# Attention's 64-row query block moved from the end of the sequence to its start, and shorter fills of the expert rows

## The chip, the cores and the metric

The kernel runs on one core of a Trainium2 chip. The metric is the device time of one execution in microseconds (us); below it the profile's own span, from the first to the last instruction, is used to read where the time lies. TensorE is called PE in the profile (PEld is its weight load), VectorE DVE, ScalarE ACT, GpSimd POOL, and SyncE, which issues most transfers, SP.

## The reference

Three layers run one after the other, all in float32. The change touches the first one and the scratch rows of the second.

```python
# attention: B, H, S, D = 4, 8, 576, 64
scores = scale * q @ k.T                      # scale = 1/sqrt(D)
cum = cumsum(maximum(s, 0), axis=-1)
bias = -(cum[:, :, :, None] - cum[:, :, None, :])
scores = where(causal, -1e9, scores + minimum(bias, 0.0))
attn = softmax(scores)                        # with + 1e-9 in the denominator
x = (attn @ v) -> rows of 512                 # B * S = 2304 rows
# mixture of experts: one of 8 experts for each row
e = argmax(x @ w_gate); y = gate * (relu(x @ w1[e]) @ w2[e])
# gated layer
out = (silu(xn @ w_gate) * (xn @ w_val)) @ w_out      # xn: y normalized by its rms
```

The sequence has 576 = 4.5 x 128 rows, and a query row sees only the keys up to its own place.

## The kernel before

The 32 heads are worked in 16 pairs `p`, two heads `h` side by side in the 128 partitions (64 for each head). For each pair these steps run, each a function that issues instructions of one kind:

- `attn_load`, `load_bias`, `load_v`: SP's transfers of q, k, the cumulated `s` (broadcast over partitions: `sums` for the full blocks, `cm` for the short block) and v.
- `mask_sums`, `q_diag`: on POOL, from pair 2 on, the causal mask is added to the bias, and the short block's queries of both heads are laid out block-diagonally (`bd`).
- `s_mm` (with `s_start`): PE makes the scores of a query block `i`, and DVE reads them from PSUM, adds the bias and takes the row's extreme (`reduced`, line 298). The full blocks 0 to 3 (128 rows each) see 128, 256, 384 and 512 keys; each is a pair of matmuls, one for each head, which contract over that head's 64 partitions. The short block `sm` (block 4, rows 512 to 575) puts 64 rows of either head into one block of 128 rows and contracts over all 128 partitions; it sees all 576 keys, in two halves of 288.
- `s_exp`: ACT's nine exponentials of a pair. `s_norm`: the reciprocals of the sums, on DVE.
- `t_mm`: PE transposes the probabilities in 25 blocks of 128 x 128, gathered in seven PSUM tiles t0 to t6, and ACT copies them to `pt` in ten copies (line 406).
- `pv_mm`: the product with v, `pvy` for rows 64 to 575 and `pvx` for the first 64, over five key blocks j. `pv_out`: two copies on ACT. `o_mm`: PE multiplies by identity and gate weights (`tl`), DVE scales into `xt` and `lp`.

The order on PE, ACT, DVE and SP is the order of the code: `attention` makes a plan of (time, function) from the tables `POS`, `TURN` and others, in units in which a pair is 10 long, sorts it and issues. Steps of different pairs overlap: PE runs the scores of pair p+1, then the transposes of pair p, then `sm` of p+1, then the product of pair p. PSUM has eight banks under one tag, and every tile takes one in turn, so a tile waits until the one eight places ahead has been read.

`route` (one call for each of the four batches) ranks the rows by expert and scatters them with an indirect DMA on POOL to `xs`, in which each expert has its own region. Before that `prefill` writes empty rows at the head of each of the eight regions: 384 rows (`FILLR`) from one row of zeros, `zrow`. The next stage reads at most 312 rows (`CAP[0]`) of a region other than the first.

After attention the expert stage runs on PE (lines 915 and 938), then the gated layer (lines 1320, 1713 and 1778).

## Time and profile before

| | |
|---|---|
| median of 3 runs | 839.19 us (838.82 to 839.22) |
| the profiled execution's own time | 838.61 us |
| its span, first to last instruction | 836.9 us |
| mean granted TensorE clock | 0.994 of full |
| PE / DVE / ACT / POOL busy | 98% / 76% / 55% / 27% of the span |

Attention takes about the first 180 us of the span. What is outside the span is 838.61 - 836.9 = 1.7 us. Busy time of PE is modelled: neighbouring matmuls overlap, so the time that a group costs is read from the chain of waits or from the distance between starts rather than from the sum of its instructions.

### The profile page before, as it was taken

The page shows a single profiled execution, that of the slowest core. Times are in us where ns is not written, and L with a number is a line of the kernel's source. Part 1 is how long each engine was busy: PE and PEld are TensorE (multiplying, and loading weights), DVE is VectorE, ACT ScalarE, POOL GpSimd, SP SyncE. Part 2 cuts the span into 40 slices and gives each one's busy share as a digit, 9 for nine tenths or more (in the row PEclk, how much of TensorE's full clock was granted, in tenths as well). Part 3 has the DMA queues.
Part 4 walks back from the last instruction along what each step waited for, and adds up shares of the span by engine and source line. Part 5 has one row for each costly group of instructions (what it writes and reads, how often), then busy time and mean ns, then how long its engine had stood idle before and what let it go on. Part 6 is the DMA issues. An engine that isn't in the chain of part 4 may idle for free.

```text
span 836.9 us, 15788 instructions
## 1 busy us (share of the span) xinstructions
PE 816.7 (98%) x5622; PEld 746.7 (89%) x5622; DVE 639.6 (76%) x1425; ACT 461.9 (55%) x1060; POOL 227.0 (27%) x249
## 2 busy tenths in 40 slices
PE   7999999999999999999999999999999999999994
PEld 4777767789899999999999999999999998899994
DVE  6657688965866768777698988988888869868880
ACT  5988989865756656566543433333333334553440
POOL 3335856332000000000221233444343351031120
PEclk9999999999999999999999999999999999999997
DMA  7999989236567566767661332322222376344510
GB/s 226 299 320 314 315 245 295 84 126 214 193 193 245 179 228 204 237 206 233 225 197 66 131 109 103 131 94 98 104 100 99 108 282 191 81 151 146 159 52 29
DMA packets 79757, 146.72 MB, mean 175 GB/s; under 512 B 7424, under 2 KB 44315, under 8 KB 79667
## 3 DMA queue, kind: packets, MB, share of 16 engines
q1 hardware_dynamic: 76707, 136.08, 51.4%
q0 software_dynamic: 2912, 9.46, 3.0%
q8 instruction: 46, 0.75, 0.4%
q14 instruction: 44, 0.36, 0.1%
q10 hardware_dynamic: 48, 0.07, 0.0%
HBM read 108.04 MB, written 37.54 MB: 174 GB/s over the span
## 4 chain that ended last, share of the span: by engine, by line
PE 92%; DVE 3%; ACT 2%; DMA 1%; issue 1%; SPq 0%; POOL 0%; POOLq 0%; DVEq 0%; ACTq 0%
PE gg L1320 29%; PE g L938 12%; PE g L915 12%; PE gp L1778 10%; PE go L1713 6%; PE pvy L419 5%; PE t L373 5%; PE s L310 5%; PE tl L447 2%; PE sm L341 1%; PE xp L886 1%; ACT pt L406 1%; DMA ringa<-ytd 1%; PE r L987 1%; PE r L976 1%
## 5 line engine op out<-in xcount | busy, mean ns | idle before, releaser
L938 PE MATMUL g<-h,u 128*128 128x256 f32 (+7 forms) x768 | 104.3, 294 | 0.0
L915 PE MATMUL g<-xt,u 128*128 128x256 f32 (+7 forms) x768 | 103.9, 294 | 0.0
L915 PEld LDWEIGHTS g<-xt,u 128*128 128x128 f32 x768 | 101.0, 188 | 0.8
L938 PEld LDWEIGHTS g<-h,u 128*128 128x128 f32 x768 | 100.5, 188 | 0.5
L1297 POOL TENSOR_TENSOR ws<-raw,ws 128x512 fp32r<-128x512 f32 (+1 forms) x25 | 33.0, 1335 | 219.4 <-ACT ws L1292 219.4
L747 ACT CAST u<-raw 128x1024 fp32r<-128x1024 f32 x62 | 65.1, 1050 | 20.9 <-DMA raw<-in_w 20.9
L354 ACT ACTIVATE p<-sc,nm 128x128 f32<-128x128 f32 (+3 forms) x128 | 71.2, 581 | 6.0 <-DVE nm L298 6.0
L760 DVE TENSOR_TENSOR u<-raw,u 128x1024 fp32r<-128x1024 f32 x58 | 70.3, 1216 | 0.9 <-ACT u L747 0.9
L1320 PE MATMUL gg<-gx2a,ws 128*128 128x384 f32 x360 | 67.4, 335 | 0.6 <-DVE tmp L1342 0.6
L1320 PE MATMUL gg<-gx0a,ws 128*128 128x384 f32 x360 | 67.7, 336 | 0.0
L1320 PE MATMUL gg<-gx1a,ws 128*128 128x384 f32 x360 | 67.1, 335 | 0.0
L1320 PEld LDWEIGHTS gg<-gx2a,ws 128*128 128x128 f32 x360 | 62.8, 188 | 0.9 <-DVE tmp L1342 0.9
L1320 PEld LDWEIGHTS gg<-gx0a,ws 128*128 128x128 f32 x360 | 63.1, 188 | 0.0
L1320 PEld LDWEIGHTS gg<-gx1a,ws 128*128 128x128 f32 x360 | 62.7, 188 | 0.0
L1358 POOL TENSOR_TENSOR hs<-tmp,hs 128x384 f32<-128x384 f32 x27 | 30.3, 1122 | 106.2 <-ACT hs L1356 106.2
L406 ACT COPY pt<-t 128x512 f32<-128x512 f32 (+3 forms) x160 | 56.0, 451 | 3.0 <-PE t L373 2.0
L373 PE MATMUL t<-ident,p 128*128 128x128 f32 x400 | 52.1, 275 | 0.1
L373 PEld LDWEIGHTS t<-ident,p 128*128 128x128 f32 x400 | 44.5, 140 | 8.5 <-DVE nm L298 8.3
L1699 POOL DMA_INDIRECT out<-raw,oid x18 | 20.5, 1138 | 112.1 <-DVE raw L1800 64.5
L419 PE MATMUL pvy<-pt,vp 128*64 128x512 f32 (+4 forms) x320 | 47.5, 428 | 0.9 <-ACT pt L406 0.9
L1338 ACT COPY tmp<-gg 128x384 f32<-128x384 f32 x27 | 13.0, 482 | 57.1 <-PE gg L1320 55.4
L1248 ACT ACTIVATE raw<-raw 128x512 f32<-128x512 f32 x31 | 21.1, 681 | 36.0 <-DVE raw L1246 35.8
(391 smaller groups left out, 1809.5 us busy)
## 6 DMA issues: line engine op xcount, KB each, us to landing
raw<-in_w SPq DMA_DIRECT2D x64, 512.0 KB
hd<-hs SPq DMA_DIRECT2D x72, 192.0 KB
xs<-zrow SPq DMA_DIRECT2D x8, 771.0 KB
raw<-in_wo SPq DMA_DIRECT2D x12, 512.0 KB
raw<-in_wg SPq DMA_DIRECT2D x12, 512.0 KB
raw<-in_wv SPq DMA_DIRECT2D x12, 512.0 KB
vp<-in_v SPq DMA_DIRECT2D x16, 320.0 KB
in<-cumd SPq DMA_DIRECT2D x20, 256.0 KB
```

Of the source, the lines that this page charges most:

```text
L310: k.nc.tensor.matmul(ps[h], st.q[r, 128 * i:128 * i + 128], st.k[r, 0:w], start=True, stop=p >= BYPE)
L354: k.nc.scalar.activation(out, st.s[i, h][:, 0:w], AF.Exp, bias=st.nm[:, n:n + 1], scale=-1.0, accum_out=acc)
L373: nc.tensor.transpose(ps[:, off:off + 128], src[:, 128 * j:128 * j + 128], k.ident)
L406: nc.scalar.copy(b, a)
L419: nc.tensor.matmul(st.y[r, a - 64:512], st.v[:, h, j, :], k.pt[:, h, o:o + S - a], start=j == 0, stop=j == 4)
L747: nc.scalar.copy(w[:, :, 0, :], raw)
L760: k.nc.vector.tensor_tensor(w[:, :, 1, :], raw, w[:, :, 0, :].bitcast(F32), op=ALU.subtract)
L915: nc.tensor.matmul(ps[:, 0:n], w[:, f % 4, a, 128 * kc:128 * kc + 128], x[b][:, kc, 0:n], start=kc == 0 and i == 0, stop=kc == 3 and i == 2)
L938: nc.tensor.matmul(ps[:, 0:n], w[:, f % 4, a, 128 * c:128 * c + 128], k.h[b][:, f, 0:n], start=f == 0 and i == 0, stop=f == 7 and i == 2)
L1320: k.nc.tensor.matmul(k.ps[u, bank], w[:, a, 128 * c:128 * c + 128], x[:, b, GT * c:GT * c + GT], start=first and c == 0 and n == 0, stop=c ...
L1713: k.nc.tensor.matmul(k.acc[tau], c[:, a, 128 * t:128 * t + 128], w[:, b, :], start=f == 0 and i == 0, stop=f == NF - 1 and i == 2)
L1778: k.nc.tensor.matmul(k.acc[i, bank], t[:, a, j, :], item_weight(k, j, w, b), start=first and j == 0 and n == 0, stop=j == 5 and n == 2, sk ...
```

## The change

The short block becomes block 0: queries 0 to 63, which see 64 keys. The full blocks become 1 to 4 and start 64 rows in, so that they see 192, 320, 448 and 576 keys. The widest one does not fit into a PSUM bank and is made in two halves of 288. A half block of 64 keys is left at the end of each full block's row; head 1's probabilities are stored with their 64-key blocks in reverse order, so that the half blocks of the two heads lie side by side and are transposed together (v of head 1 is laid out to match by the host). The mask adds on POOL change with it, `cm` needs 64 instead of 576 columns, and the row tile that has only 64 rows is the first instead of the last. The tables give the steps their new order. `zrow`, `mz` and `half` move into free columns of the probability buffers. `prefill` writes 312 rows (104 partitions x 3) in seven of the eight regions.

```diff
-JB = (0, 576, 1024, 1344, 1536)
+STRIP = (1408, 0, 448, 896, 1344)
+START_OF = [128 * i * i - 128 for i in range(5)]
+UNITS64, C0, LAST = 16, 4, 13
...
+    n = CM // 3 if c else FILLR // 3
     i = nc.sync.dma_start(
-        out=k.xs[REG * c:REG * c + FILLR, :].rearrange("(a p) d -> p a d", p=128),
-        in_=k.zrow.unsqueeze(1).broadcast_to((128, FILLR // 128, XROW)),
+        out=k.xs[REG * c:REG * c + 3 * n, :].rearrange("(a p) d -> p a d", p=n),
+        in_=k.zrow[0:n].unsqueeze(1).broadcast_to((n, 3, XROW)),
...
     if n == 0:
-        in_turn(k, G.tensor_tensor(cb[:, :, 0:2, :], cb[:, :, 3:1:-1, :], m.unsqueeze(1).broadcast_to(sh), op=ALU.add))
-        in_turn(k, G.tensor_tensor(cb[:, :, 5, :], cb[:, :, 5, :], m.broadcast_to((128, 2, 128)), op=ALU.add))
+        in_turn(k, add(cb[:, :, LAST:16, :], cb[:, :, C0:C0 + 3, :], 1))
+        in_turn(k, add(cb[:, :, C0 - 1::-1, :], cb[:, :, C0 + 1:C0 + 5, :], 0))
+        in_turn(k, add(cb[:, :, C0 + 7:LAST, :], cb[:, :, C0 + 7:LAST, :], 2))
...
-        k.nc.sync.dma_start(out=st.cm[64 * h:64 * h + 64, :], in_=k.cumd[2 * p + h:2 * p + h + 1, :].broadcast_to((64, S)))
+        k.nc.sync.dma_start(out=st.cm[64 * h:64 * h + 64, :], in_=k.cumd[2 * p + h:2 * p + h + 1, 0:64].broadcast_to((64, 64)))
...
+def width(i):
+    return 64 + 128 * i
...
+def s_start(k, p, i, c=0, w=None):
+    st, w = k.st[p], w or width(i)
+    q = slice(128 * i - 64, 128 * i + 64)
+    ps = st.ps[i, c] = [bank(k, f"s{p}_{i}_{c}_{h}", w) for h in range(2)]
     for h, r in enumerate(ROWS2):
-        k.nc.tensor.matmul(ps[h], st.q[r, 128 * i:128 * i + 128], st.k[r, 0:w], start=True, stop=p >= BYPE)
+        k.nc.tensor.matmul(ps[h], st.q[r, q], st.k[r, c:c + w], start=True, stop=p >= BYPE or c + w < width(i))
...
     if i == 0:
+        ps = bank(k, f"sm{p}", 64)
+        nc.tensor.matmul(ps, st.bd, st.k[:, 0:64], start=True, stop=False)
+        nc.tensor.matmul(ps, k.identb, k.mask[:, 0, 0:64], start=False, stop=True)
+        reduced(k, scores(0)[:, 0:64], ps, st.cm, acc(10))
...
+    else:
+        for c in (HALF, 0):
+            s_start(k, p, 4, c, HALF)
...
-            ps = k.psum.tile([128, 512], F32, name=f"sm{p}_{n}", tag="b")[:, 0:HALF]
-            nc.tensor.matmul(ps, st.bd, st.k[:, c], start=True, stop=n == 0)
...
+        if h:
+            out, src = (t.rearrange("p (b n) -> p b n", n=64) for t in (out, src))
+            out = out[:, ::-1, :]
...
-TURN = dict(S=(0, 1, 3, 2, 4), X=(0, 1, 2, 3, 6, 7, 4, 5, 8))
+TURN = dict(S=(1, 2, 4, 3, 0), X=(0, 1, 2, 3, 6, 7, 4, 5, 8))
```

Three places show what moves. First PE's matmuls for the scores of pair 2, before (a row names the tile written, with block and head, and its shape; `in` holds q and k):

```order
L310 MATMUL s_0_0_430<-in_143 128x128
L310 MATMUL s_0_1_431<-in_143 128x128
L310 MATMUL s_1_0_439<-in_143 128x256
L310 MATMUL s_1_1_440<-in_143 128x256
L310 MATMUL s_3_0_454<-in_143 128x512
L310 MATMUL s_3_1_455<-in_143 128x512
L310 MATMUL s_2_0_462<-in_143 128x384
L310 MATMUL s_2_1_463<-in_143 128x384
...
L341 MATMUL sm_0_535<-in_143 128x288
L341 MATMUL sm_1_538<-in_143 128x288
L343 MATMUL sm_1_538<-mask,identb 128x64
```

The same steps of pair 2 on PE after the change (a full block's third number is the first key of the half):

```order
L328 MATMUL s_1_0_0_441<-in_144 128x192
L328 MATMUL s_1_0_1_442<-in_144 128x192
L328 MATMUL s_2_0_0_450<-in_144 128x320
L328 MATMUL s_2_0_1_451<-in_144 128x320
L328 MATMUL s_4_288_0_464<-in_144 128x288
L328 MATMUL s_4_288_1_465<-in_144 128x288
L328 MATMUL s_4_0_0_468<-in_144 128x288
L328 MATMUL s_4_0_1_469<-in_144 128x288
L328 MATMUL s_3_0_0_481<-in_144 128x448
L328 MATMUL s_3_0_1_482<-in_144 128x448
...
L354 MATMUL sm_553<-in_144 128x64
L355 MATMUL sm_553<-mask,identb 128x64
```

Per head the full blocks go from 1280 to 1536 columns and from four tiles to five; the short block goes from 2 x 288 to 64 columns. Next ACT's copies of the transposed probabilities of pair 1 to `pt`, before:

```order
L406 COPY pt_154<-t_1_488 128x512
L406 COPY pt_154<-t_2_495 128x384
L406 COPY pt_154<-t_3_502 128x384
L406 COPY pt_154<-t_4_507 128x2x256
L406 COPY pt_154<-t_5_513 128x2x128
L406 COPY pt_154<-t_5_513 128x2x2x64
L406 COPY pt_154<-t_6_520 128x2x64 x3
```

And after the change:

```order
L453 COPY pt_149<-t_1_507 128x512
L453 COPY pt_149<-t_2_514 128x384
L453 COPY pt_149<-t_3_521 128x384
L453 COPY pt_149<-t_4_526 128x2x256
L453 COPY pt_149<-t_5_532 128x2x128
L453 COPY pt_149<-t_5_532 64x64 x2
L453 COPY pt_149<-t_6_539 64x4x64 x2
```

With the copy of t0 ahead of these rows it is ten copies before and after. Before, `pvy`'s first matmul pair (j = 0, 512 columns) read t0, t1 and the second copy of t5; after, it reads t0 and t1 alone, `pvx` reads the small copies of t5, and j = 1 is the first that reads t6. Last POOL's mask adds of one pair (pair 4), before:

```order
L249 TENSOR_TENSOR cb_148<-cb_148,mz 128x2x256
L250 TENSOR_TENSOR cb_148<-cb_148,mz 128x2x128
L253 TENSOR_TENSOR cb_148<-cb_148,mz 128x256 x2
...
L249 TENSOR_TENSOR in_142<-in_142,mz 128x2x256
L250 TENSOR_TENSOR in_142<-in_142,mz 128x2x128
```

And after:

```order
L258 TENSOR_TENSOR cb_147<-cb_147,p_129 128x2x192
L258 TENSOR_TENSOR cb_147<-cb_147,p_129 128x2x4x64
L258 TENSOR_TENSOR cb_147<-cb_147,p_129 128x2x128
...
L259 TENSOR_TENSOR cb_147<-cb_147,p_129 128x128 x2
L293 TENSOR_TENSOR in_144<-in_144,p_129 128x128
```

The adds ahead of the pair's scores become three (384, 512 and 256 columns) instead of two (512 and 256); the two that stand between a pair's reductions shrink from 256 to 128 columns.

## Rows read from the trace of the kernel before

**Rows 1.** The page: busy time, and the span in 40 slices.

```profile
PE 816.7 (98%) x5622; PEld 746.7 (89%) x5622; DVE 639.6 (76%) x1425; ACT 461.9 (55%) x1060; POOL 227.0 (27%) x249
...
DMA  7999989236567566767661332322222376344510
```

**Rows 2.** Busy time by windows: attention, one stretch of it, the expert stage.

```profile
20.00:180.00 160.00, 158.71 (x1237) 112.86 (x1236) 115.93 (x498) 144.30 (x458) 82.12 (x90) 1.00 0.86 263
80.00:100.00 20.00, 19.70 (x152) 13.83 (x150) 11.99 (x55) 19.02 (x60) 16.20 (x17) 1.00 1.00 330
300.00:470.00 170.00, 170.00 (x1215) 167.50 (x1214) 133.13 (x206) 95.05 (x185) 18.00 (x14) 1.00 0.59 191
```

**Rows 3.** The chain of waits over one pair: start, duration, what.

```profile
162.17 2.36 PE s L310 x16
...
167.14 0.76 PE t L373 x7
...
168.40 0.97 PE sm L341 x4
169.37 0.03 PE sm L343
169.40 0.33 PE tl L447 x2
169.72 1.01 PE pvy L419 x4
170.73 0.12 PE pvx L423 x4
170.85 1.73 PE pvy L419 x16
172.58 0.26 PE t L373
```

**Rows 4.** The timeline at an ordinary pair's scores, from 43.6 us.

```profile
43.76 2.43 PE L310 MATMUL s<-in,in 64*128 64x128 f32 x16
...
44.42 0.29 DVE L298 CUSTOM_DVE_ANT_0 sc<-s,cb 128x128 f32<-128x128 f32 x1 [1.95 <-PE s L310]
...
44.85 0.42 DVE L298 CUSTOM_DVE_ANT_1 sc<-s,cb 128x256 f32<-128x256 f32 x1
```

**Rows 5.** The timeline at a pair whose bias came late, from 64.7 us.

```profile
64.72 2.43 PE L310 MATMUL s<-in 64*128 64x128 f32 x16
...
65.10 1.27 POOL L249 TENSOR_TENSOR in<-in,mz 128x512 f32<-128x512 f32 x1 [6.70 <-DMA in<-cumd]
...
66.41 0.29 DVE L298 CUSTOM_DVE_ANT_0 sc<-s,in 128x128 f32<-128x128 f32 x1 [2.59 <-POOL in L249]
```

**Rows 6.** Groups of instructions by form, 23.4 to 180 us: PEld, PE, ACT, POOL.

```profile
L373 PEld LDWEIGHTS t<-ident,p 128*128 128x128 f32 x375 | 41.8, 141 | 8.4 <-DVE nm L298 8.3
...
L419 PE MATMUL pvy<-pt,vp 128*64 128x512 f32 x60 | 16.2, 618 | 0.7 <-ACT pt L406 0.7
...
L354 ACT ACTIVATE p<-sc,nm 128x512 f32<-128x512 f32 x28 | 21.6, 770 | 0.0
...
L354 ACT ACTIVATE p<-sc,nm 128x128 f32<-128x128 f32 x28 | 11.1, 404 | 4.7 <-DVE nm L298 4.7
...
L250 POOL TENSOR_TENSOR in<-in,mz 128x256 f32<-128x256 f32 x10 | 7.4, 738 | 0.0
```

**Rows 7.** The chain of waits at the start, 12 to 22 us.

```profile
15.10 2.71 ACT p L354 x11
17.81 2.72 ACT pt L406 x7
...
20.58 1.08 PE pvy L419 x4
```

**Rows 8.** The page, DMA issues: KB each.

```profile
xs<-zrow SPq DMA_DIRECT2D x8, 771.0 KB
...
in<-cumd SPq DMA_DIRECT2D x22, 144.0 KB
```

More of the change, by code (lines that the diff above doesn't have):

```diff
@@ L158, in cumulate @@
     yield
-    for i in range(2):
+    for i in (1, 2):
         s_start(k, 0, i)
@@ new lines, in scores, with acc @@
+    def scores(h):
+        sc = st.s[i, h] = A.tile([128, S], F32, name=f"sc{p}_{i}_{h}", tag="sc", bufs=4)
+        return sc
+    def acc(n):
+        return st.nm[:, n:n + 1]
+    if i == 1:
+        st.nm = A.tile([128, 12], F32, name=f"nm{p}", tag="nm", bufs=3)
+    w = width(i)
+    if i == 0:
+        ps = bank(k, f"sm{p}", 64)
+        nc.tensor.matmul(ps, st.bd, st.k[:, 0:64], start=True, stop=False)
+        nc.tensor.matmul(ps, k.identb, k.mask[:, 0, 0:64], start=False, stop=True)
+        reduced(k, scores(0)[:, 0:64], ps, st.cm, acc(10))
+    elif i < 4:
+        if (i, 0) not in st.ps:
+            s_start(k, p, i)
+        ps = st.ps.pop((i, 0))
+        if p < BYPE:
+            mask_pe(k, ps, w)
+        for h in range(2):
+            sc, a = scores(h)[:, 0:w], acc(2 * i - 2 + h)
+            c = st.cb[:, h]
+            if p < BYPE or i == 3:
+                reduced(k, sc, ps[h], sums(st, h)[:, 0:w], a)
+            elif i == 1:
+                reduced(k, sc, ps[h], flat(c[:, LAST:16, :]), a)
+            else:
+                reduced(k, *(t.rearrange("p (b n) -> p b n", n=64) for t in (sc, ps[h])), c[:, C0::-1, :], a)
+    else:
+        for c in (HALF, 0):
+            s_start(k, p, 4, c, HALF)
+        if p < BYPE:
+            mask_pe(k, st.ps[4, HALF], HALF)
+        sc = [scores(h) for h in range(2)]
+        for c in (HALF, 0):
+            ps = st.ps.pop((4, c))
+            for h in range(2):
+                reduced(k, sc[h][:, c:c + HALF], ps[h], sums(st, h)[:, c:c + HALF], acc((8 if c else 6) + h))
+                if c and p >= BYPE:
+                    mask_sums(k, p, 1 + h)
+        nc.vector.tensor_tensor(st.nm[:, 6:8], st.nm[:, 6:8], st.nm[:, 8:10], op=ALU.min)
@@ L387, in t_mm, with both @@
+    def both(a, n):
+        return ps[:, a:a + 2 * n].rearrange("p (h n) -> p h n", h=2)
+    ev = []
+    if g < 4:
+        j, h = divmod(g, 2)
+        for i in range(j + 1, 5):
+            tr(128 * (i - j - 1), i, h, j)
+        n = 512 - 128 * j
+        a = STRIP[j] + 64
+        ev.append((ps[:, 0:n], pt[:, h, a:a + n]))
     elif g == 4:
         for h in range(2):
-            for i in range(2, 4):
-                tr(256 * h + 128 * (i - 2), ph[i][h], 2)
-        ev.append(both(0, 4, JB[2]))
+            for i in (3, 4):
+                tr(256 * h + 128 * (i - 3), i, h, 2)
+        ev.append((both(0, 256), pt[:, :, STRIP[2] + 64:STRIP[2] + 320]))
@@ new lines, in t_mm @@
+        nc.tensor.transpose(ps[0:64, 256:384], pm, k.ident)
+        ev.append((both(0, 128), pt[:, :, STRIP[3] + 64:STRIP[3] + 192]))
+        for h in range(2):
+            ev.append((ps[0:64, 256 + 64 * h:320 + 64 * h], pt[64 * h:64 * h + 64, h, STRIP[0]:STRIP[0] + 64]))
+    else:
+        for i in range(1, 5):
+            a = START_OF[i] + 128 * i
+            nc.tensor.transpose(ps[:, 128 * i - 128:128 * i], ph[:, a:a + 128], k.ident)
+        for h in range(2):
+            ev.append((ps[64 * h:64 * h + 64, :].rearrange("p (i n) -> p i n", i=4)[:, :, 64:128],
+                       pt[64 * h:64 * h + 64, h, 0:1792].rearrange("p (i n) -> p i n", i=4)[:, :, 0:64]))
```

149 lines of the change are left out of this document (60 added, 89 removed).

## The prediction

> **What bounds the kernel now.** I read the page first, then windows, then the chain of waits. On the page PE is busy for 98% of the span and no other engine for more than 76% [rows 1]; of the 160 us of attention from 20 to 180 us PE is busy for 158.71, and of 170 us in the expert stage for all 170 [rows 2]. The chain of waits shows why: over one pair of heads it stays on PE from the pair's scores to the next step of that kind, 172.58 - 162.17 = 10.41 us without a wait [rows 3]. So attention is priced by what PE issues for a pair, and a microsecond taken from PE there comes off the end, as long as what follows is PE work too. Two others stand close behind. ACT is busy for 144.30 of the 160 us, and for 19.02 of 20 us where it also casts weights [rows 2]. The transfer engines are nearly full up to some 145 us [rows 1, 2], and in one pair this shows: the bias landed late, POOL's first add began at 65.10, and DVE began to read the scores 1.69 us after PE began them (66.41 - 64.72) [rows 5], against 0.66 us in an ordinary pair (44.42 - 43.76) [rows 4].
>
> **The scores on PE.** A row that covers both heads tells that they run side by side: the product with v beyond its first tile and `pvx` is 448 + 320 + 192 + 64 = 1024 columns for each head, and takes 1.73 us, so 1.69 ns a column for the two heads together; `sm`, which uses all 128 partitions for one block, takes 0.97 us for 2 x 288 columns, so 1.68 ns a column [rows 3]. A column costs the same whether it serves one head over 64 partitions plus another beside it, or one block over 128. That is where this change acts: the exponentials, reductions and copies keep their columns (2 x 1280 + 576 = 2 x 1536 + 64), but on PE the 576 columns of the short block become 64, and the full blocks grow by 256 columns, not by 512, since both heads share them.
>
> The full blocks before: 1280 x 1.69 ns = 2.16 us of the 2.36 [rows 3], so 0.20 us are fixed. After: 1536 x 1.69 ns + 0.20 = 2.80 us, 0.44 more. The fifth tile adds next to nothing, since the four that stand now carry no more than those 0.20 together.
>
> The short block before: 0.97 + 0.03 (its mask) = 1.00 us [rows 3]. After it is one matmul of 64 columns in two passes. No row shows a pass of 64 columns with a full 128 x 128 load of weights. From below: `pvx` has 64 columns with half as wide weights, and its two passes take 0.12 us, 0.06 each [rows 3]. From above: a transpose has that weight load and 128 columns, and takes 0.76 / 7 = 0.109 us [rows 3]. I take the transpose, which has the same load of 128 x 128 in float32: 2 x 0.109 + 0.03 = 0.25 us. The lower bound is 0.15; the upper one, if the mask also waits for its weights, 0.33.
>
> The weight loads of the transposes take 141 ns each in the trace, longer than the transposes' distance, so they overlap [rows 6]. The Trainium skill, "TensorE: Matmul & The Clock Gate", section "LDWEIGHTS (loading the stationary operand)", says that a load costs its columns divided by 1.2 per ns, however few columns then stream: about 107 ns for 128. By it a pass could not go below 0.107 us, and the short block would cost 0.24; by columns alone it would cost 0.14. The 0.109 of the transposes agrees with it, but they stream 128 columns, so no row here shows which of the two limits them.
>
> A pair saves 1.00 - 0.25 - 0.44 = 0.31 us, with bounds 0.41 and 0.23. The transposes stay 25, `tl` and the product with v keep their columns. Pairs 0 and 1 have their scores in the start, which ACT bounds; the other 14 save **4.3 us** (3.2 to 5.7).
>
> **The start.** From 15.10 to 20.5 us the chain is on ACT: eleven exponential entries, then seven copies, then `pvy` [rows 7]. The four exponentials of pair 1 that stand ahead of the copies grow by 256 columns together; at (770 - 404) / 384 = 0.95 ns a column [rows 6] that is 0.24 us later. But `pvy`'s first matmuls wait for the seventh copy now and for the second after the change, so their 1.08 us [rows 7] run while the copies go on, and the next, j = 1, waits for the tenth. I estimate a gain of about half a us against the 0.24: **0.25 us**. Bounds: a gain of 0.45; a loss of 0.4, if the 128 more columns that PE makes ahead of the first reduction, at two passes and half the clock, push ACT's start back.
>
> **The waits inside attention.** In all, PE waited 0.7 us for copies ahead of `pvy` [rows 6]. The same shift of the copies can take this away; bank waits (below) can add as much. I take 0, between -0.8 and +0.8.
>
> **What costs nothing, and its cover.** ACT and DVE get the same columns; DVE one more reduction a pair, with 44.1 us of idle time in those 160 [rows 2]. POOL's mask adds grow from 512 + 256 to 384 + 512 + 256 columns ahead of a pair: at 1.27 us for 512 [rows 5] and 0.74 for 256 [rows 6] about 3.0 us instead of 2.0, issued most of a pair ahead, on an engine that is half idle. Without that cover the second block's reduction comes 1 us later, in that pair alone. `cm` shrinks from 144 KB [rows 8] to 16, twice a pair, and `sums` grows by 64 columns. The seven fills lose 72 rows of 2056 bytes each, 1.04 MB in all, from 771 KB each [rows 8]. None of these transfers is on the chain [rows 3], so the fills are worth 0 here.
>
> Sum: 4.3 + 0.25 = 4.55 us. Against its own execution 838.61 becomes 834.1, with a span of 832.3 instead of 836.9. The median of the runs is 0.58 above that execution: 839.19 - 4.55 = **834.6 us**.
>
> **The rivals.**
>
> Late bias. Where the bias comes late now it may come late more often, since PE reaches each pair sooner. For: the engines are nearly full, and 1.69 us is past what the new order bears (next rival). Against: each pair loads some 190 KB less, 0.6 us at 300 GB/s, while PE takes 0.31 from it. If some three pairs lose 0.35 us each, the time is 835.6. The Trainium skill, "DMA: Bandwidth & Descriptors", section "Why a DMA increments its semaphore by 16 and not by 1", says that a transfer runs on the largest number of engines up to 16 that divides its outer size: 104 partitions would run on 13, so that each still writes 24 rows, as with 128 on 16, and the fills would hold the queue as long as before. No row of the trace before shows a fill of 104 partitions.
>
> PSUM banks (slower). A pair's scores take ten tiles and there are eight banks, so block 3 waits until DVE has read block 1. PE gets there 1088 columns into the pair, 1088 x 1.69 ns + 0.1 = 1.95 us. DVE starts at 0.66 + 64 x 1.69 ns = 0.77 and needs two reductions of about (0.29 + 0.42) / 2 = 0.36 us [rows 4]: free at 1.48, 0.47 us in hand. With the late pair's 1.69 [rows 5] it is 2.40, a wait of 0.45. If that were the case in all 14 pairs, 6.3 us would outweigh the 4.55: **841.0 us**. It decides from a DVE start of about 1.55 us, where the wait eats a pair's 0.31. Against: 0.66 us is the ordinary case [rows 4], in the late one the add itself took 1.27 us of the delay, and the first add now has 384 columns and ends 0.27 us sooner. The Trainium skill, "TensorEngine Tiling (Array Packing)", section "Gotcha 1: PSUM Pressure", warns that row tiles write to different banks and so raise the pressure on PSUM. No row before shows ten tiles in one group.
>
> Reversed writes. ACT now writes head 1's probabilities with blocks in reverse, 1536 columns a pair. If these cost twice the 0.95 ns, ACT gets 1.46 us more a pair, 20 us in 14, and its 144.3 would be 164.7, more than the 160 now: about 844 us. It decides from some 0.5 us a pair. Against: nothing in the trace makes such a pattern slow; DVE reads its bias with blocks in reverse already (the 256-column form) at 0.42 [rows 4], on the line of the plain ones. For: no ACT row writes backwards.
>
> Given back later. The expert stage starts 4.5 us earlier, and if its first weights or rows are then late, all is lost: 839.2. Against: that stage's PE is busy without a gap [rows 2], and its loads are freed by PE's own progress.
>
> **How the numbers follow.** The forecast has 0.76, late bias 0.08, banks 0.05, reversed writes 0.05, given back later 0.06. A measurement here tells 0.2%, 1.7 us, from no change. Faster: 0.76 + 0.08 + 0.01 of mild forms of the others = 0.85; same 0.07; slower 0.08. The forecast's own best is 5.7 + 0.45 + 0.8 = 7.0 us, 832.2; its worst 3.2 - 0.4 - 0.8 = 2.0, 837.2. I widen the upper end to 838.0 for mild forms of banks and late bias, and the lower one to 832.0 for rounding.
>
> **What the profile after would show.** Right: the scores of a pair at 2.80 us in the chain, `sm` with its mask at 0.25, and a period of 10.1. `sm` at 0.15 or 0.33 decides the weight load. Waits of PE for DVE ahead of block 3 would be the banks; exponentials of head 1 longer than head 0's of the same width the reversed writes; POOL waiting for transfers the late bias; the first expert matmul earlier but the end unmoved the last rival. What would make me wrong is a wait that I read as slack.

## The result, and the profile after

The changed kernel takes 846.74 us (median of 5 runs, 844.09 to 848.19) where the kernel before takes 839.19 (5 runs on the same chip, 838.48 to 840.25). The ratio is 1.0081 with a 95% interval of 1.007 to 1.0093: 7.5 us slower, where 4.6 us faster was forecast. The profiled execution took 846.74 us with a span of 844.9, 8.0 longer than before. Chips differ (the kernel before had medians from 839 to 846 us on those used below), so each experiment has a ratio to the kernel before on its own chip.

The page of the kernel after, its span, busy times, the granted clock and the transfer engines by slices (to compare with [rows 1]):

```profile
span 844.9 us, 15907 instructions
...
PE 820.8 (97%) x5654; PEld 753.9 (89%) x5654; DVE 643.8 (76%) x1457; ACT 468.5 (55%) x1060; POOL 235.0 (28%) x270
...
PEclk9999999999999999999999999999999999999998
DMA  6996757543576667677671433322333364544510
```

Busy times by windows of the kernel after, attention, and four windows of 2 us in it (columns: window, length, PE, PEld, DVE, ACT, POOL, granted clock, DMA share, GB/s):

```profile
20.00:180.00 160.00, 153.27 (x1194) 113.04 (x1193) 117.49 (x518) 143.89 (x439) 83.42 (x102) 0.98 0.69 227
...
40.00:42.00 2.00, 0.44 (x4) 0.22 (x2) 0.00 (x0) 0.87 (x2) 2.00 (x3) 1.00 0.96 330
42.00:44.00 2.00, 0.68 (x4) 0.41 (x5) 1.35 (x6) 0.00 (x0) 1.48 (x4) 0.91 0.96 331
44.00:46.00 2.00, 2.00 (x10) 2.00 (x11) 0.82 (x5) 1.55 (x6) 0.00 (x0) 0.50 0.98 268
46.00:48.00 2.00, 2.00 (x15) 1.14 (x16) 0.95 (x4) 2.00 (x6) 0.00 (x0) 0.74 0.96 338
```

PE is no longer without gaps: 153.27 of 160 us instead of 158.71 [rows 2]. From 40 to 42 us PE is busy for 0.44 us, ACT for 0.87 and DVE not at all, while POOL is busy for the whole 2 us, and from 44 to 46, when PE is busy again, the granted clock is 0.50, its lower level.

Where the time went is seen in the distance from one pair's first matmul of the product with v to the next pair's, worked out from the starts of these matmuls (us; the first product starts at 20.58, 20.98, 20.74 and 20.90; the last two kernels are experiments below):

| interval | before | after | adds_after_diag | one_decode |
|---|---|---|---|---|
| 1st | 9.91 | 10.87 | 10.67 | 10.68 |
| 2nd | 10.41 | 15.04 | 10.51 | 10.50 |
| 3rd to 6th, 11th to 13th, sum of 7 | 73.87 | 71.79 | 71.29 | 71.28 |
| 7th to 10th, sum of 4 | 43.88 | 49.30 | 46.69 | 45.23 |
| 14th | 11.01 | 10.91 | 11.43 | 11.45 |
| sum | 149.08 | 157.91 | 150.59 | 149.14 |

The expert stage's first matmul comes at 191.50 instead of 182.26: 9.24 later, of which 8.83 are the sum and 0.40 the start; from there to the end the two executions take 653.4 and 654.6, so that 8.0 are left in the span. Two intervals lose 10.05 us together, the 2nd (15.04 against 10.41) and the 9th (15.90 against 10.48). An ordinary pair is faster, as forecast.

**An ordinary pair.** The chain of waits of the kernel after over one pair, to set beside [rows 3]:

```profile
57.04 1.01 PE pvy L466 x4
58.05 0.12 PE pvx L470 x4
58.17 1.73 PE pvy L466 x16
59.90 2.83 PE s L328 x20
62.73 1.35 PE t L420 x11
...
66.59 0.17 PE sm L354 x2
66.76 0.03 PE sm L355
66.79 0.33 PE tl L494 x2
67.12 0.57 PE pvy L466
```

The period is 67.12 - 57.04 = 10.08 us against 10.41, so 0.33 saved where 0.31 was forecast. The full blocks' scores take 2.83 us (forecast 2.80), the short block 0.17 + 0.03 = 0.20 (forecast 0.25, between 0.15 and 0.33).

**The first stall.** The timeline of the kernel after from 38 to 46 us, POOL, DVE and PE (in brackets the idle time before, and what ended it; L258 are the next pair's three mask adds, L259 the pair's own two, L307 a reduction):

```profile
39.29 2.90 POOL L258 TENSOR_TENSOR cb<-cb,p 128x384 f32<-128x384 f32 x3 [8.97 <-DMA cb<-cumd]
42.14 0.88 POOL L259 TENSOR_TENSOR in<-in,p 128x128 f32<-128x128 f32 x2
...
42.64 0.63 DVE L307 CUSTOM_DVE_ANT_0 sc<-s,in 128x448 f32<-128x448 f32 x1 [4.02 <-POOL in L259]
...
43.33 0.44 PE L420 MATMUL t<-ident,p 128*128 128x128 f32 x2 [2.88 <-DVE nm L307]
```

The chain of waits at the same place:

```profile
39.43 0.78 PE t L420 x7
40.21 0.04 issue
40.24 1.95 POOL cb L258 x2
42.19 0.42 POOL in L259
...
42.64 0.07 DVE sc L307
...
43.33 0.44 PE t L420 x2
```

POOL works in the order of its code. Its next instruction is an add to `cb`, the bias of the next pair, and that bias has not landed: POOL waits 8.97 us for it. Behind it in the queue stand the adds to `in`, which the pair at work needs now, and whose bias has long been there. DVE's reduction of block 3 waits 4.02 us for them, and PE's transposes wait 2.88 us. In the kernel before, the bias of this `cb` was later still, its add beginning at 42.04:

```profile
42.04 1.28 POOL L249 TENSOR_TENSOR cb<-cb,mz 128x512 f32<-128x512 f32 x1 [2.27 <-DMA cb<-cumd]
43.27 0.73 POOL L250 TENSOR_TENSOR cb<-cb,mz 128x256 f32<-128x256 f32 x1
45.42 1.42 POOL L253 TENSOR_TENSOR cb<-cb,mz 128x256 f32<-128x256 f32 x2 [1.42 <-DVE nm L298]
```

That is the timeline of POOL in the kernel before, and nothing stood behind the waiting adds but their own pair's. The plan tells why. The next pair's adds are due at `MASK` = -9.7 of their own pair, so 0.3 of the plan's units into this one. The own adds are issued with a block's reductions: with block 1's before (`if i == 1`), at 0.2; with the first half of the widest block's now (`if c and p >= BYPE`), at 0.81. So the two groups have changed places in POOL's queue, though `MASK` was not touched. POOL's instructions of the kernel after, in order:

```
L258 TENSOR_TENSOR cb_147<-cb_147,p_129 128x2x192
L258 TENSOR_TENSOR cb_147<-cb_147,p_129 128x2x4x64
L258 TENSOR_TENSOR cb_147<-cb_147,p_129 128x2x128
L259 TENSOR_TENSOR in_143<-in_143,p_129 128x128 x2
L293 TENSOR_TENSOR p_129<-in_143,p_129 128x128
L258 TENSOR_TENSOR in_144<-in_144,p_129 128x2x192
L258 TENSOR_TENSOR in_144<-in_144,p_129 128x2x4x64
L258 TENSOR_TENSOR in_144<-in_144,p_129 128x2x128
L259 TENSOR_TENSOR cb_147<-cb_147,p_129 128x128 x2
```

Between the two groups of `cb_147` stands the group of `in_144`, the next pair's. The wait costs more than its length: the same interval takes 10.51 us in adds_after_diag, where POOL's order is put right, so it is 15.04 - 10.51 = 4.53 us longer for 2.88 us of waiting.

**The second stall.** The timeline of the kernel after from 106 us (L796 is POOL's part of splitting the gate weights, L1292 and L1293 DVE's decode of an output weight):

```profile
108.61 2.92 POOL L258 TENSOR_TENSOR in<-in,p 128x384 f32<-128x384 f32 x3 [2.14 <-DMA in<-cumd]
111.47 4.88 POOL L796 TENSOR_TENSOR u<-raw,u 128x1024 fp32r<-128x1024 f32 x2
...
113.09 1.05 DVE L1292 TENSOR_SCALAR raw<-raw 128x512 uint32<-128x512 uint32 x1
114.18 2.72 DVE L1293 SCALAR_TENSOR_TENSOR raw<-raw 128x512 uint32<-128x512 uint32 x1
...
117.69 1.84 PE L328 MATMUL s<-in,in 64*128 64x288 f32 x6 [2.23 <-DVE nm L307]
```

The same work in the kernel before:

```profile
102.68 4.69 POOL L749 TENSOR_TENSOR u<-raw,u 128x1024 fp32r<-128x1024 f32 x2
...
108.35 0.70 DVE L1246 SCALAR_TENSOR_TENSOR raw<-raw 128x512 uint32<-128x512 uint32 x1
```

POOL waits 2.14 us for another bias, so its weight job begins after it, at 111.47, and lies beside DVE's decode; the same decode step takes 2.72 us instead of 0.70, the reductions queued behind it on DVE are late, and PE waits 2.23 us for a bank. Before, the job was over at 107.4, ahead of the decode; in the kernel after ACT had cast the job's two inputs at 107.39 and 110.06, so with POOL free it would, by an estimate from its 2.35 us for each, have been over at some 112.4, ahead of it too. The same interval takes 12.38 us in adds_after_diag, so the stall makes it 15.90 - 12.38 = 3.52 longer, and not the whole difference from an ordinary pair: 2.30 us stay without it.

### The profile page after: what moved, and what is told of

Read it like the earlier page. It is cut to its first block, busy times and chain, and to the rows that moved or that the text cites. A ratio compares the mean times of both kernels' runs of the same rounds, so it can differ in the third digit from the quotient of the medians.

```text
span 844.9 us, 15907 instructions
## 1 busy us (share of the span) xinstructions
PE 820.8 (97%) x5654; PEld 753.9 (89%) x5654; DVE 643.8 (76%) x1457; ACT 468.5 (55%) x1060; POOL 235.0 (28%) x270
## 4 chain that ended last, share of the span: by engine, by line
PE 90%; DVE 4%; ACT 2%; DMA 1%; issue 1%; POOL 0%; SPq 0%; POOLq 0%; DVEq 0%; ACTq 0%
PE gg L1367 29%; PE g L985 12%; PE g L962 12%; PE gp L1825 10%; PE go L1760 6%; PE s L328 5%; PE pvy L466 5%; PE t L420 4%; PE tl L494 2%; PE xp L933 1%; ACT pt L453 1%; DMA ringa<-ytd 1%; ACT p L400 1%; PE t L448 1%; PE r L1034 1%
## 5 line engine op out<-in xcount | busy, mean ns | idle before, releaser
L400 ACT ACTIVATE p<-sc,nm 128x192 f32<-128x192 f32 (+2 forms) x144 | 82.8, 577 | 6.4 <-DVE nm L307 4.2
L453 ACT COPY pt<-t 128x512 f32<-128x512 f32 (+4 forms) x160 | 60.2, 429 | 9.6 <-PE t L420 4.9
L307 DVE CUSTOM_DVE_ANT_0 sc<-s,in 128x288 f32<-128x288 f32 (+3 forms) x90 | 38.2, 470 | 17.8 <-PE s L328 9.2
L466 PE MATMUL pvy<-pt,vp 128*64 128x448 f32 (+4 forms) x320 | 49.0, 430 | 0.2
L420 PEld LDWEIGHTS t<-ident,p 128*128 128x128 f32 x320 | 36.9, 144 | 13.2 <-DVE nm L307 11.1
L420 PE MATMUL t<-ident,p 128*128 128x128 f32 x320 | 44.5, 281 | 3.2 <-DVE nm L307 3.2
```

The lines of the kernel that those rows point to most:

```text
L400: k.nc.scalar.activation(out, src, AF.Exp, bias=st.nm[:, at:at + 1], scale=-1.0, accum_out=acc)
L420: nc.tensor.transpose(ps[:, off:off + 128], ph[:, a:a + 128], k.ident)
L453: nc.scalar.copy(b, a)
L466: nc.tensor.matmul(st.y[r, a - 64:512], st.v[:, h, j, :], k.pt[:, h, o:o + S - a], start=j == 0, stop=j == 4)
```

## The experiments

The theory after reading this: POOL's queue order makes the stalls, and the clock that falls after each wait adds to them. Rivals: the shorter fills do something to the queue of transfers; ACT or DVE has become the bound; the start. The runs on one chip are 1 to 4, 5 to 8, 9 and 10, 11 and 12, 13 to 15, and 16.

**1 to 4. Order or fills.** The changed kernel with the own adds ahead of the next pair's again:

```diff
-MASK = -9.7
+MASK = -9.1
```

> The changed kernel with one number moved, so that on POOL the two small adds that a pair's own block 3 needs stand ahead of the next pair's three adds again, as they do in the kernel before. Theory A (POOL's queue): DVE no longer waits at 41 us for adds that stand behind a bias transfer, and POOL's long weight job no longer slides under DVE's work at 113 us, so both stalls go. The 15 intervals from pair to pair were 157.9 us after the change and 149.1 before; without the two long ones (15.04 and 15.90 in place of 10.08) they are 147.1, and the time is 746.7 less than the changed kernel's by about 10: 836 to 838 us, faster than before by 1 to 3. Theory B (the fills of 104 partitions hold the transfers up, and late bias is the cause): the bias still lands at 39 us, PE waits for it under another name, and the time stays within 2 us of 846.7. If only the first stall goes, 841 to 842.

Measured: 848.49 us against 846.22, 1.0025 (1.0014 to 1.0035). Two thirds of the loss is gone and the 2nd interval is 10.32, but the gain that was expected with it isn't there, and ordinary pairs are 10.33 instead of 10.08. The changed kernel with fills of 384 rows:

```diff
-    n = CM // 3 if c else FILLR // 3
+    n = FILLR // 3
```

> The changed kernel with the eight fills of 384 rows from 128 partitions again. Theory A: the transfers carry 1 MB more in the first 60 us, the bias of the pair at 41 us lands no earlier than before the change (POOL began there at 42.04 before, 39.29 after), so the stall at 41 us stays or grows by up to 2.7 us: 846 to 851 us. Theory B: the fills run on all engines again, the transfers get through sooner, the wait of 2.88 us at 43 us is gone and the time falls to 840 to 843.

Measured: 852.10, 1.008 (1.0053 to 1.0107). The fills do not make the loss. The kernel before with only the fills of 312 rows, that is the change's lines in `prefill` with `n = CM // 3 if c else FILLR // 3` and nothing else of it:

> The kernel before with the change of the fills alone (312 rows from 104 partitions in seven of the eight regions). Theory A: nothing waits for these transfers on the path, 839.2 within 0.8 us. Theory B: the slower fills make the bias late here too; POOL's wait for it at 42 us grows, PE waits, and the time is 842 to 846.

Measured: 846.15, 0.9996 (0.9982 to 1.0009): no gain or loss by the fills is seen. And the kernel before, otherwise untouched, with the next pair's adds ahead of the own ones:

```diff
-MASK = -9.7
+MASK = -9.85
```

> The kernel before with one number moved, so that on POOL the next pair's two adds stand ahead of the two that the pair's own blocks need, as they do after the change. Theory A: at 35 us the own adds now wait for a bias that lands at 42 us and for 2.0 us of adds, so DVE and then PE stop for some 4 to 6 us, and the clock falls after it: 844 to 850 us. Theory B: the order does nothing as long as the transfers are on time as they are in this kernel: 839 to 840.

Measured: 858.39, 1.0145 (1.0119 to 1.0171), with PE waiting 2.51 us at 31 and 4.88 us at 69. The order of two groups of adds on an engine busy for 27% of the span makes a kernel 12.2 us slower without any other part of the change. This and the first run settle the queue.

Why were ordinary pairs slower in own_first? Its timeline from 57.5 us, POOL's adds and the minimum over the two halves of the widest block (L384):

```profile
61.48 2.94 POOL L258 TENSOR_TENSOR in<-in,p 128x384 f32<-128x384 f32 x3
...
61.61 0.90 DVE L384 TENSOR_TENSOR nm<-nm 128x2 f32<-128x2 f32 x1
62.43 0.61 DVE L307 CUSTOM_DVE_ANT_0 sc<-s,in 128x448 f32<-128x448 f32 x1
```

The minimum of 128 x 2 numbers takes 0.16 us when POOL is idle (at 38.45 us in the kernel after), and 0.34 in that kernel's ordinary pairs, beside POOL's layout of `bd`. Here it begins just behind POOL's first add (61.48, 1.01 us long) and ends at 62.51, just when that add does (62.49). The Trainium skill, "SBUF — State Buffer", section "SBUF: two separate sides", says that DVE and GpSimd share one pair of ports, which an instruction of DVE with two inputs in SBUF (or in a 2-port mode) and one of GpSimd take as an exclusive lock: whichever starts first has it for its whole length, and the other waits. The trace agrees here, and at the decode above, where POOL's second piece ran until 116.35 and DVE's step ended 0.55 us later. The reductions of 288 columns, which read scores from PSUM, took 0.45 us beside POOL's own adds as without them.

**5 to 8. The second stall, and the minimum.** own_first with the minimum moved behind the reductions of block 3; the adds moved behind the layout of `bd`, far from the minimum; the changed kernel with the decode at another place; and the first with that decode:

```diff
+        if i == 3:
+            nc.vector.tensor_tensor(st.nm[:, 6:8], st.nm[:, 6:8], st.nm[:, 8:10], op=ALU.min)
...
-        nc.vector.tensor_tensor(st.nm[:, 6:8], st.nm[:, 6:8], st.nm[:, 8:10], op=ALU.min)
```

> The kernel with the pair's own adds first, and one DVE instruction more in another place: the minimum over the two halves of block 4 (128x2, line 384) stands behind block 3's reductions instead of ahead of them. In the profile with the own adds first, this small instruction took 0.90 us while POOL ran its first add of 1.00 us, and 0.34 us after the change, where POOL was idle; block 3's banks came free later, and a pair took 10.33 us, 10.08 after the change. Theory C (a small DVE instruction is held while POOL works, and here it stands on the path): the period falls to 10.08 in some 10 pairs, 2.5 us, ratio to the kernel before 0.998 to 1.000 after 1.0025. Theory D (eight banks for ten tiles: the transposes wait because the scores take ten banks, whatever stands between the reductions): the period stays at 10.3, ratio 1.002 to 1.003.

```diff
-MASK = -9.7
+MASK = -3.9
```

> The changed kernel with the next pair's three adds moved further back on POOL, behind its own adds and behind the block-diagonal copy too. Theory C: POOL's adds now run later in the pair, beside DVE's sums and reciprocals instead of the minimum, which falls from 0.90 to 0.34 us, while the scaling of the sums grows from 0.2 to 0.6 us where nothing waits for it; period 10.08, ratio 0.998 to 1.000. Theory D: 10.3 and 1.002 to 1.003, as with the own adds first. If the adds come so late that the next pair's reductions wait for them, more than 10.3.

```diff
-            add(at + (7.25 if n == 1 else 6.3), out_first, k, 4 + n)
+            add(at + 11.0, out_first, k, 4 + n)
```

> The changed kernel, POOL's order unchanged, with DVE's decode steps (lines 1292 to 1294) of five places moved behind the scores' reductions of the pair instead of ahead of them. If the second stall, 2.23 us before 117.69 us, comes from the decode step that took 2.72 us beside POOL's weight job, it goes, with the slow clock behind it: 5 us less than the changed kernel, ratio 1.002 to 1.003 in place of 1.008, and the first stall at 41 us stays as it is. If it comes from POOL's order or late bias, the reductions still wait there and the ratio stays at 1.006 to 1.008.

> Three moves together: own adds first, the minimum behind block 3, the decode steps behind the reductions. If the three waits are separate, this is the change as it was priced, with the slower start: the intervals between pairs at 10.08 apart from those with routing steps, 1 to 3 us faster than the kernel before, ratio 0.996 to 0.999. If they share a cause that is still there (banks, late bias), 1.001 or more.

Measured, against 840.13 us: own_late_min 841.72, 1.0019 (1.0009 to 1.003), ordinary pairs 10.07; adds_after_diag 840.49, 1.0011 (1.0001 to 1.0021), both stalls gone; decode_later 847.60, 1.0101 (1.0078 to 1.0124), which took the stall out of the 9th interval (11.53) and made one of 14.93 in the 10th, DVE being late for the routing (PE waited 2.73 us for its rows at 125.58); own_min_decode 845.43, 1.0064 (1.0046 to 1.0083), likewise worse. So one number, the place of POOL's adds, takes 7.0 of the 8.1 thousandths back (8.1 measured on another chip). The gain that was forecast, and expected of own_late_min and adds_after_diag, still doesn't come.

**9 and 10. The start and the routing.** adds_after_diag with the blocks of the first two pairs in another order, and that with the routing's steps spread out:

```diff
+FIRST = dict(S=(1, 2, 3, 4, 0), X=(0, 1, 2, 3, 4, 6, 5, 7, 8))
...
-                for i, at in zip(TURN.get(tag, range(9)), POS[tag]):
+                for i, at in zip((FIRST if p < BYPE else TURN).get(tag, range(9)), POS[tag]):
```

> The kernel with POOL's adds behind the block-diagonal copy, and for the first two pairs alone the blocks in the order 1, 2, 3, 4, 0 (exponentials in the same order). Theory E (the start): after the change ACT stood for 1.65 us at 12 us, until block 4's four reductions of 288 columns and the minimum were done (13.72), where the kernel before waited 0.63 + 0.27 us (13.28), and pvx and pvy then waited for the last copies. With block 3 ahead, its exponential can start after one reduction of 0.62 us: ACT's chain starts some 0.6 us sooner and the first product with v at 20.1 to 20.4 instead of 20.74; the ratio falls by 0.0005 to 0.001 from 1.0011. Rival: the start hangs on PE at half clock, and nothing changes.

```diff
-                    add(10 * p + ROUTE[0] + ROUTE[1] * n, step, j)
+                    add(10 * p + ROUTE[0] + (ROUTE[1] if p > 7 else 0.4) * n, step, j)
```

> The kernel with the start in the new order, and the routing steps of the first two batches spread over almost two pairs (0.40 instead of 0.22 of a tenth of a pair from one step to the next). Theory F (DVE is the bound in the pairs with routing): in the kernel with POOL's adds behind the copy, DVE was busy for 10.37 of 12.5 and 12.52 of 13.0 us in the two pairs from 105.5 to 131 us, which took 12.38 and 13.02 us where 10.48 and 11.78 were taken before. With the steps spread, the two together fall from 25.4 to 22 to 23.5 us, and the ratio to 0.997 to 0.999. Rival G (eight banks for ten tiles): the pairs stay long wherever a decode step delays the first reduction, the sum stays over 24.5 and the ratio within 0.001 of the start's.

Measured, against 843.70: 845.33, 1.0018 (1.0005 to 1.003), and 847.61, 1.0046 (1.003 to 1.0063). With the new order the first interval is 10.22 and the first product comes at 22.68 instead of 20.74, but that can't be put down to the order: casts_early below, whose start is unchanged, shows 10.22 and 22.95, and route_spread, with the new order, 10.75 and 21.36. The times show no gain. Spread steps put the scatters ahead of a pair's own adds on POOL, where DVE then waited 3.68 us and PE 3.22: the queue again.

**11 to 16. What eats the rest.** With both stalls gone the pairs near 93 to 131 us are long. Windows of adds_after_diag, three of these pairs and an ordinary one:

```profile
93.00:105.50 12.50, 12.34 (x89) 8.51 (x87) 7.09 (x31) 12.35 (x36) 9.88 (x9) 1.00 0.70 232
105.50:118.00 12.50, 12.02 (x88) 8.75 (x90) 10.37 (x37) 11.77 (x36) 7.80 (x8) 1.00 0.44 144
118.00:131.00 13.00, 11.51 (x94) 8.04 (x92) 12.52 (x57) 10.67 (x34) 5.83 (x8) 1.00 0.60 188
57.00:67.00 10.00, 10.00 (x84) 7.58 (x83) 6.96 (x32) 9.62 (x31) 4.24 (x6) 1.00 0.97 328
```

ACT is busy for 12.35 of 12.50 us where it casts weights, and for 9.62 of 10 even in an ordinary pair; DVE is busy for 12.52 of 13.00 where decode and routing meet. I read from this that a pair there is ACT's or DVE's, not PE's, by the rival "an engine has become the bound". The test moves ACT's casts (1.07 us each) to DVE (0.64 each), at several places; each diff is against adds_after_diag, casts_early's against casts_on_dve, one_decode's against casts_earlier:

```diff
-PIECES = (81.8, 84.0, 91.8, 94.0, 159.0, 161.7)
+PIECES = (84.3, 85.3, 94.3, 95.3, 159.0, 161.7)
...
-            add(at, split, k, 1, n in (0, 1, 4, 5), n in (4, 5))
+            add(at, split, k, 1, n in (0, 1, 4, 5), True)
```

> The kernel with POOL's adds behind the block-diagonal copy, and the four weight casts of 1.07 us each that ACT made in two pairs (at 92.56 to 103.98 us) moved to DVE, into the stretch ahead of the short block's reduction where DVE was idle for 3 us. Theory H (ACT is the bound where it casts): there pvx and the second step of the product with v came 0.6 us later than in an ordinary pair (1.58 and 1.79 us after the product's start instead of 1.02), and the two pairs took 11.23 and 12.38 us. Without the casts the first falls to 10.1 to 10.3 and the second to 11.0 to 11.8, some 2 us together, ratio 0.998 to 0.9995 after 1.0011. Rival: DVE, with a decode step in the second pair, has no room for them; the second pair stays at 12.4 or grows, and the ratio at 1.000 to 1.002.

```diff
-EARLY_P, EARLY_OUT = 9, 5
+EARLY_P, EARLY_OUT = 11, 4
```

> The same, and the early decoding of output weights begins two pairs later and takes four pieces instead of five (the fifth is decoded in the expert stage with the others), so that DVE has no decode step in the pair with the casts and one less beside the first routing. Theory F (DVE is the bound where routing and decoding meet): the pairs from 104 to 131 us, 12.38 and 13.02, fall to 10.3 and 12 together with the casts, ratio 0.9965 to 0.9985. Rival G (eight banks for ten tiles): the pair with routing stays at 13.0 since its reductions start late anyhow, and the ratio is no more than 0.001 under the run with the casts alone. If the fifth piece is late in the expert stage, PE waits there instead.

```diff
-PIECES = (81.8, 84.0, 91.8, 94.0, 159.0, 161.7)
+PIECES = (84.3, 85.3, 91.8, 94.0, 159.0, 161.7)
...
-            add(at, split, k, 1, n in (0, 1, 4, 5), n in (4, 5))
+            add(at, split, k, 1, n in (0, 1, 4, 5), n not in (2, 3))
...
-            add(at + (7.25 if n == 1 else 6.3), out_first, k, 4 + n)
+            add(at + (5.4 if n < 2 else 6.3), out_first, k, 4 + n)
```

> The kernel with POOL's adds behind the block-diagonal copy, two of the four weight casts on DVE (in the first of the two pairs, which has no decode step), and the first two decode steps moved ahead of the short block's reduction, into the stretch where DVE stood idle for 3 us. Theories F and H (the saving of the change went into three pairs in which ACT casts or DVE decodes and routes): the pairs of 11.23, 12.38 and 13.02 us become 10.1 to 10.6, 11 to 11.8 and 11.5 to 12.3, 2.5 to 4 us together, and the kernel is faster than the one before the change, ratio 0.996 to 0.9985. If the saving is lost elsewhere (start, or after attention), the ratio stays at 1.000 or more with those pairs shortened.

The unchanged kernel after, on the same chip:

> The changed kernel as it is, on the chip of the run beside it. If its two stalls (2.88 us at 43 us and 2.23 us at 118 us) come from the order of the instructions, they stand at the same places again and the ratio is 1.007 to 1.010; if they were an accident of one execution, they don't.

```diff
-PIECES = (81.8, 84.0, 91.8, 94.0, 159.0, 161.7)
+PIECES = (74.3, 75.3, 84.3, 85.3, 159.0, 161.7)
...
-            add(at + (7.25 if n == 1 else 6.3), out_first, k, 4 + n)
+            add(at + (5.4 if n < 2 else 6.3), out_first, k, 4 + n)
```

(all casts of `split` on DVE, as in casts_on_dve)

> The kernel with POOL's adds behind the block-diagonal copy, all four weight casts on DVE (0.64 us each there) and a pair earlier, and the first two decode steps ahead of the short block's reduction. In the run before this one the first decode step fell beside POOL's weight job (5.38 us) and took 2.74 + 2.48 us for 0.69 + 0.43; here that job is done a pair earlier. Theories C, F and H: the decode step takes 0.7 us again, the pairs of 12.61 and 13.70 us become 10.1 to 10.6 and 11.5 to 12.5, and the time falls under that of the kernel before, ratio 0.9955 to 0.9985. If the rest of the saving is lost elsewhere, the ratio stays at 0.9995 or more.

```diff
-            add(at + (5.4 if n < 2 else 6.3), out_first, k, 4 + n)
+            add(at + (5.4, 7.25, 6.3, 6.3, 6.3)[n], out_first, k, 4 + n)
```

> The run before this one with its second decode step at its old place again, behind the routing's first steps. There it stood ahead of them, PE waited 2.31 us for the routing's one-hot rows and the clock fell after it: that pair took 15.90 us, the two before it 10.03 and 10.08. Theories F and H: the pair takes some 13.0 us as with POOL's adds behind the copy alone, 2.9 us less, and the kernel is faster than the one before the change, ratio 0.995 to 0.9975. If the time does not follow the pair, the rest of the saving is lost elsewhere, and the ratio stays at 0.999 to 1.000.

| run | us | before, same chip | ratio (95%) |
|---|---|---|---|
| casts_on_dve | 845.08 | 844.72 | 1.0001 (0.999 to 1.0012) |
| casts_early | 846.12 | 844.72 | 1.0018 (1.0003 to 1.0034) |
| two_casts_decode | 840.79 | 840.64 | 0.9999 (0.999 to 1.0008) |
| after_again | 846.99 | 840.64 | 1.0072 (1.0057 to 1.0088) |
| casts_earlier | 839.88 | 840.36 | 0.9993 (0.9984 to 1.0002) |
| one_decode | 838.11 | 839.43 | 0.9987 (0.9978 to 0.9996) |

after_again repeats the loss on another chip, with both waits in the same places (1.95 us at 42.62, 2.33 at 117.17). Without ACT's first casts (casts_on_dve) the pair that had them falls from 11.23 to 10.08 us, and the one ahead of it, where DVE now casts, goes from 10.06 to 10.64: the sum is 0.57 less, as an ACT bound says. casts_early, which takes the decode out of these pairs as well, has 10.12, 10.08, 10.08 and 11.81 in the 7th to 10th: 42.09 in all, 4.60 less than adds_after_diag and 1.79 less than the kernel before, 0.45 for each pair. So it was the casts and the decode that took the saving there. But each version met a new wait: casts_early has 14.25 in the 11th, where DVE decodes now and everything is released late (last section), 12.94 in the 14th, and a wait of 2.21 us in the expert stage at 403; casts_on_dve and two_casts_decode met one at the port; in casts_earlier and one_decode, with POOL's weight job a pair earlier, the 7th interval grew from 10.06 to 12.12 and 12.13, POOL being busy for 11.89 of the 12 us from 83 to 95 (one_decode), where PE waited 1.63 us. The timeline of two_casts_decode, POOL's weight job and DVE's decode:

```profile
103.11 5.38 POOL L796 TENSOR_TENSOR u<-raw,u 128x1024 fp32r<-128x1024 f32 x2
...
103.51 2.74 DVE L1293 SCALAR_TENSOR_TENSOR raw<-raw 128x512 uint32<-128x512 uint32 x1
106.28 2.48 DVE L1294 TENSOR_SCALAR raw<-raw 128x512 uint32<-128x512 uint32 x1
```

These steps take 0.69 and 0.43 us where POOL is idle. one_decode is the one version whose whole interval lies under 1: 1.3 us faster than the kernel before, but it is the best of thirteen versions, so the 95% are to be taken with care. Its profile doesn't show where: its intervals sum to 149.14 us against 149.08 before, its expert stage begins at 182.65 against 182.26, and its span is 836.3 against 836.9, so the 0.6 that these two executions differ lies behind attention, where other profiles of these kernels differ by as much. That stays open, and so does what the same moves would give the kernel before, which was not tried.

## Why the prediction was wrong

**Right: the scores.** 2.83 us, 0.20 and a period of 10.08 are within 0.05 of the forecast. The price of a transpose, 0.109 us, was too dear for a pass: two passes of `sm` took 0.17, 0.085 each. The Trainium skill, "TensorE: Matmul & The Clock Gate", section "LDWEIGHTS (loading the stationary operand)", gives a load the time of its columns divided by 1.2 per ns; the estimate from it, at least 0.107 us for a pass, is above these 0.085, and the measurement decides. In the seven intervals that the table sums, away from the stalls and the casts, the kernel in which the stalls are gone saves 73.87 - 71.29 = 2.58 us, 0.37 each.

**Right: what costs nothing.** The fills cost and gave nothing (0.9996). Reversed writes: the 448-column exponentials of both heads take 0.65 us, so the order costs nothing. Bank waits: none in an ordinary pair; the second stall ends in one (2.23 us), which the decode made.

**Wrong: POOL's cover.** The step that failed is in "What costs nothing, and its cover": the mask adds are "issued most of a pair ahead, on an engine that is half idle", and without that cover "the second block's reduction comes 1 us later, in that pair alone". I priced POOL as capacity, by idle time and the length of its adds. It is a queue: what counts is what stands behind an instruction that waits for a transfer. The adds of the next pair wait for a bias up to 8.97 us, and since the change the pair at work stands behind them. The swap stood in the order of POOL's instructions: of the kernel after, the section on the change shows a pair's first three adds and its two own ones with a gap marked between them, and in that gap are the next pair's three. I read the rows for their widths and not for what lay between. And [rows 5] show a wait of 6.70 us for a bias: enough to price a queue behind it.

**Wrong: "late bias" as a rival.** I let a late bias delay the pair that owns it, at 0.35 us, and gave it 0.08. It delayed the pair ahead of it. The bias itself was not later: 39.29 against 42.04.

**Wrong by size: the waits inside attention, "0, between -0.8 and +0.8".** The two stalls cost 4.53 + 3.52 = 8.05 us against the same intervals of adds_after_diag. Without them the saving is still eaten: the 7th to 10th intervals lose 46.69 - 43.88 = 2.81 us to ACT and DVE, the first 0.76 and the last 0.42, 3.99 against the 2.58 gained (adds_after_diag; with 0.10 in the 2nd that is the difference of the sums, 1.51). The forecast gave each of the 14 pairs the full 0.31, though [rows 2] showed ACT busy for 19.02 of 20 us in this very stretch: with PE quicker, ACT sets those pairs, and where the decode meets the routing DVE does. casts_early shows it: with the casts off ACT and the decode in later pairs, the same four intervals gain 1.79.

**Wrong: the start.** A gain of 0.25 was forecast, with a loss of 0.4 as its bound. The first product came 0.40 later in this execution, but that time moves from one to the next: 20.58 to 21.29 in three profiles with the start of the kernel before, 20.74 to 23.50 in those with the changed one. What repeats is the first interval, which the forecast had 0.31 shorter: 9.91 in the two profiles of the old start that no stall touches there, 10.60 to 10.87 in twelve of the thirteen with the changed start, 10.22 in the other. The chain of waits at the start of the kernel after:

```profile
13.96 1.97 ACT p L400 x5
...
16.05 3.13 ACT p L400 x13
19.18 2.55 ACT pt L453 x7
...
22.40 0.96 PE pvy L466 x2
```

The ACT chain starts at 13.96, since it waits for the four reductions of the widest block and the minimum. The first product no longer waits for the seventh copy and runs ahead, but the next step waits on the later ones, until 22.40; so from the product's start to the next scores PE takes 24.67 - 20.98 = 3.69 us instead of 23.43 - 20.58 = 2.85, and the first interval grew from 9.91 to 10.87. The step that failed is the gain of half a us for hiding the product's first part beside the copies: the wait of j = 1 for the later copies, which was named there, cost 0.84.

## What to carry to other kernels

An engine that is idle for most of the time is still a queue. When a table or a step's place changes, list for each engine what stands behind every instruction that can wait for a transfer, across the neighbouring iterations and not in one alone; a single swap there cost 6 to 12 us here. A saving on the first-placed engine counts only in those stretches where the second has slack: here the stretch with the casts on ACT and the decode on DVE took as much back (2.81 us) as seven pairs had gained (2.58). And the length of an instruction on DVE may be set by what POOL runs beside it, so both are read together before a step is moved.

## What the runs showed that was not expected

Either stall costs more than PE's wait, and by the same amount. The windows of 2 us of the kernel after behind the second (for the first they stand with the result):

```profile
118.00:120.00 2.00, 2.00 (x9) 0.92 (x6) 2.00 (x11) 1.75 (x8) 0.81 (x2) 0.68 0.54 213
120.00:122.00 2.00, 2.00 (x11) 2.00 (x10) 1.92 (x10) 1.07 (x2) 1.92 (x4) 0.50 0.04 8
122.00:124.00 2.00, 2.00 (x19) 2.00 (x18) 1.59 (x5) 1.75 (x5) 1.49 (x2) 0.97 0.00 0
```

The granted clock, 1.00 while PE waits (40 to 42 us), falls to its lower level after it has begun again. What is missing to full clock is 2 x (0.09 + 0.50 + 0.26) = 1.70 us behind the first wait and 2 x (0.32 + 0.50 + 0.03) = 1.70 behind the second. Wait and clock together are 2.88 + 1.70 = 4.58 and 2.23 + 1.70 = 3.93 us, where the intervals grew by 4.53 and 3.52. So these waits did not double: each cost its length and, by the clock, about the same 1.7 us or a little less.

While POOL issued a batch of scatters, eight profiles of the eighteen show what waited for PE released some 2 to 3.6 us late, once or twice. They are the eight of runs 1 to 4 and 9 to 12, from the three chips on which the kernel before took 843.70 to 846.22 us; none of the ten from chips where it took 839.19 to 840.64 shows it. The timeline of own_first (L588 a scatter, L328 the scores, L478 a copy of the product):

```profile
137.01 2.10 PE L328 MATMUL s<-in 64*128 64x192 f32 x14
...
138.71 0.97 POOL L588 DMA_INDIRECT xs<-xt,ix  x1 [0.31 <-issue]
...
140.86 0.59 ACT L478 COPY vp<-pvy 128x512 f32<-128x512 f32 x1 [3.12 <-remote]
141.04 0.36 DVE L307 CUSTOM_DVE_ANT_0 sc<-s,in 128x192 f32<-128x192 f32 x1 [3.55 <-remote]
```

PE had begun the first scores at 137.01 and went on with the next; ACT and DVE, on different tiles, got theirs at 140.86 and 141.04 together (remote: the trace shows no instruction that released them). The kernel before with short fills shows it as well, so it is not the change. Its cause was not tried, nor whether it makes the difference between these chips.
